# First tile re-planned and 512-byte q/k loads for two tiles of a fused attention and MLP kernel

## The chip, the cores and the metric

The kernel runs on one core of one Trainium2 chip. The metric is the device time of one execution in microseconds (us). The kernel before takes 272.12 us, the median of 13 runs (271.72 to 274.76).

## What is computed

For 4 batches, 8 heads, 768 tokens and a head width of 64, attention with a causal mask. Heads flagged in `is_retrieval` see all earlier keys, the others only the first 4 keys (sinks) and a window of 64. Its output, one row of 512 per token, goes through a layer of 2048 units with h - tanh(h) and back to 512.

```
scores = q @ k^T / 8;  stream_keep = causal & (is_sink | in_window)
scores = where(causal if head is retrieval else stream_keep, scores, -1e9)
x = softmax(scores) @ v                  # 3072 tokens x 512
h = x @ w_in                             # 3072 x 2048
out = (h - tanh(h)) @ w_out              # 3072 x 512, float32
```

## The kernel before, in words

Tokens are cut into 12 tiles of 256 (`TT`), three to a batch, and heads into 4 pairs. A unit n is one head pair of one tile. Each unit goes through these stages:

- `st_T`: TensorE transposes q and k of the pair into PSUM (`tp`, L487). One copy makes `qT`, two copies make the halves of `kz` (L473 on ScalarE, L475 on VectorE). `kz` is zero in the half that belongs to the other head, so it is cleared once (`zero_kz`, L349).
- `st_S`: scores into `sc` (L545), exp on ScalarE into `pt` (L560), and in the first group the mask on VectorE (L572 or L577: `pt` times `m4`).
- `st_A`: `pt` times values (L601), where key blocks further back than the previous one take `vf`, the values times the head's flag (L458, on GpSimd). Reciprocal and scaling on VectorE (L615, L620) give `x`.
- `st_X`: `x` transposed (L636) and copied to `xT` (L643).

The MLP of a tile has 8 units `H_unit(t, u)`: eight matmuls into `ph` (L663), tanh on ScalarE (L676), and the subtraction on VectorE (L683) into `gt`. `ph` has two banks, so the matmuls of unit u+2 wait for the subtraction of unit u. `O_mms` multiplies `gt` by `w_out` (L699) in groups of 16 matmuls, one group per 128 tokens, into `po`. ScalarE scales it out (L712), and SyncE (SP) stores it (L719). The output matmuls of tile t stand among the hidden units of tile t+1.

Loads: q, k and v come as float32, 256 bytes (one token of one head) to a packet (L253, on SP's queue), and are cast to 16 bits (L406 on ScalarE, L408 on VectorE or GpSimd). The six raw buffers are reused, so the loads of tile t+2 wait for the casts of tile t. The weights are loaded and cast by GpSimd's queue (L268, L280). Tiles 0 and 1 are loaded in halves of four heads.

Order: nothing is issued where it is written. Every operation is handed to `Plan.op` with an engine, a cost in ns, and what it reads and writes. `Plan.run` (L56) then plays these costs through: each engine takes, of what is ready, the operation that was recorded first. The operations are emitted in that order, and each engine runs them strictly in it. `port=True` marks operations that share GpSimd's port in the plan. A dependence named only for the plan (as `w_after` in the weight loads) makes no wait on the chip. On the chip an engine waits for the operations whose data it reads or overwrites; two readers of one tile in PSUM on different engines go one after the other as well.

The prologue stands at L748 to L781: casts of tile 0, its four units, casts of tile 1 (mostly GpSimd), the weight loads, `scale_v` (the `vf` products), and the clearing of the second `kz`. The main loop follows at L806: per hidden unit of tile t it places a share of the attention of later tiles. Tile 1's attention falls beside the hidden units of tile 0, when no output matmuls exist yet.

PSUM has eight banks: `sc` 2 x 2 banks (also used by `tp`), `m` 1 (`av`, `xp`), `h` 2 (`ph`), `o` 1 (`po`; `xp` in the prologue).

Of the kernel before, what the change touches and what calls it, by code (L numbers as in the profile page):

```python
# [16 lines left out]
class Plan:  # L17
# [3 lines left out]

    ENGINES = ("PE", "ACT", "DVE", "POOL", "SP")
    OVERLAP = {"PE": 0, "ACT": 100, "DVE": 88, "POOL": 60, "SP": 0}
    RESULT = {"PE": 200, "ACT": 0, "DVE": 0, "POOL": 0, "SP": 0}

    def __init__(self, bufs):
# [6 lines left out]
    def op(self, eng, ns, fn, r=(), w=(), dma=None, prio=None, port=False):  # L33
        i = len(self.ops)
        deps = set()
        for k in r:
            if k in self.writer:
                deps.add(self.writer[k])
            self.readers.setdefault(k, []).append(i)
        for k in w:  # L40
            if k in self.writer:
                deps.add(self.writer[k])
            deps.update(self.readers.get(k, ()))
            self.writer[k] = i
            self.readers[k] = []
        for key in (*r, *w):
            if isinstance(key, tuple) and key[0] in self.bufs:
                tag, at = key[:2]
                deps.update(self.users.get((tag, at - self.bufs[tag]), ()))
                self.users.setdefault((tag, at), []).append(i)  # L50
        deps.discard(i)
        port = port or (eng == "POOL" and not dma)
        self.ops.append((eng, ns, fn, deps, dma, i if prio is None else prio, port))
        return i
# [92 lines left out]
def kernel(  # L147
# [84 lines left out]
    raws = {}  # L232

    HH = H // 2

    def load(t, names="qkv", halves=(None,)):

        b, g = divmod(t, NG)
        for half in halves:
            h0, nh = (0, H) if half is None else (half * HH, HH)  # L240
            for nm in names:
                src = {"q": q, "k": k, "v": v}[nm]
                if (nm, t) not in raws:
                    idx = rot["raw"] = rot.get("raw", -1) + 1
                    raws[nm, t] = (
                        lazy(raw_pool, [128, NB, H, D], FP32, "raw", f"raw_{nm}{t}"), idx
                    )
                r, idx = raws[nm, t]
                for i in range(NB):
                    s0 = g * TT + i * 128  # L250
                    op(
                        "SP", max(420, 128 * nh * 1.1),
                        lambda r=r, i=i, src=src, s0=s0, h0=h0, nh=nh: nc.sync.dma_start(  # L253
                            out=r()[:, i, h0 : h0 + nh, :],
                            in_=src[b, h0 : h0 + nh, s0 : s0 + 128, :].rearrange("h p d -> p h d"),
                        ),
                        w=[("raw", idx, i, x) for x in (range(2) if half is None else (half,))],
                        dma=(128 * nh, 21.0),
                    )
# [16 lines left out]
    def load_w_out(j, w_after):  # L276
# [11 lines left out]

    retr_i = const.tile([128, 2 * H], I32, name="retr_i")
    op(  # L290
        "ACT", 400,
        lambda: nc.scalar.dma_start(
            out=retr_i[:], in_=is_retrieval.bitcast(I32).partition_broadcast(128)
        ),
        w=["retr"], dma=(128, 20.0),
# [55 lines left out]
        )  # L351

    for hp in range(HP):
        zero_kz("DVE", 0, hp, 0, S)

    nz = const.tile([128, 2 * H], FP32, name="nz")
    op(
# [52 lines left out]
    def cast_qk(t, engines, halves=range(2)):  # L410

        for half in halves:
            for nm, es in zip("qk", engines):
                if (nm, t) not in t16s:
                    t16s[nm, t] = lazy(
                        t16_pool, [128, NB, H, D], FP16, f"t16{nm}", f"t16_{nm}{t}"
                    )
                c = t16s[nm, t]
                r, slot = raws[nm, t]
                hs = slice(half * HH, half * HH + HH)  # L420
                cast_op(
                    es[half], NB * HH * D, lambda c=c, hs=hs: c()[:, :, hs, :],
                    lambda r=r, hs=hs: r()[:, :, hs, :],
                    r=[("raw", slot, i, half) for i in range(NB)], w=[("t16" + nm, t, half)],
                )

# [24 lines left out]
    def scale_v(t):  # L451
        b, g = divmod(t, NG)
        v1, vf, lo = v1s[b], vfs[b], g * NB
        for jb in range(lo, min(lo + NB, 4)):
            fl = rflag0 if jb == 0 else rflag
            op(
                "POOL", 1053,
                lambda jb=jb, fl=fl: nc.gpsimd.tensor_mul(  # L458
                    out=vf()[:, jb, :, :], in0=v1()[:, jb, :, :],
                    in1=fl[:].unsqueeze(2).to_broadcast([128, H, D + 1]),  # L460
                ),
                r=[("v1", b, g, 0), ("v1", b, g, 1), "rflag0", "rflag"], w=[("vf", b, jb)],
            )


# [5 lines left out]
    def copy(e, dst, src):  # L471
        if e == "ACT":
            nc.scalar.copy(out=dst, in_=src)  # L473
        else:
            nc.vector.tensor_copy(out=dst, in_=src)  # L475

    def st_T(n, eq="DVE", ek=("DVE", "DVE")):
        t, hp = divmod(n, HP)
        b, g = divmod(t, NG)
        cs = slice(g * TT, (g + 1) * TT)  # L480
        tp, key = bank([128, 2, NB, 128], FP16, "sc", f"tp{n}")
        cq, ck = t16s["q", t], t16s["k", t]

        def mm():
# [6 lines left out]

        op(
            "PE", 224, mm,
            r=["ident"] + [("t16" + nm, t, hp * 2 // HP) for nm in "qk"], w=[key],
        )
        qT[n] = lazy(qt_pool, [128, TT], FP16, f"qT{hp}", f"qT{n}")

        cost = {"ACT": 373, "DVE": 288}
        kk = kz[b % 2][hp]
        op(  # L500
            eq, cost[eq],
            lambda: copy(eq, qT[n]()[:], tp()[:, 0, :, :].rearrange("p i c -> p (i c)")),
            r=[key], w=[(f"qT{hp}", t)],
        )
        for hh in range(2):
            p_ = slice(64 * hh, 64 * hh + 64)
            op(
                ek[hh], cost[ek[hh]],
                lambda p_=p_, hh=hh: copy(
                    ek[hh], kk[p_, hh, cs], tp()[p_, 1, :, :].rearrange("p i c -> p (i c)")  # L510
                ),
                r=[key], w=[("kz", b % 2, hp, g)],
            )


# [137 lines left out]
    def H_unit(t, u):  # L653
# [33 lines left out]
            r=[key, tk], w=[("gt", t, u)],  # L687
        )

    def O_mms(t, j0, j1):  # L690
        for j in range(j0, j1, 2):
            ts, fb = divmod(j, NFB)
            if fb == 0:
                pos[t] = bank([128, DM], FP32, "o", f"po{t}_{ts}")
            po, key = pos[t]

            def mm(fb=fb, ts=ts, po=po):
                for f in (fb, fb + 1):
                    nc.tensor.matmul(  # L699
                        out=po()[:], lhsT=gts[t]()[:, f, ts * 128 : ts * 128 + 128],  # L700
                        rhs=w_out_t[f // 4]()[:, f % 4, :],
                        start=(f == 0), stop=(f == NFB - 1),
                    )

            op("PE", 2 * 216, mm, r=[("wout", fb // 4), ("gt", t, fb // FU)], w=[key])
            if fb == NFB - 2:
                ot = lazy(o_pool, [128, DM], FP32, "ot", f"ot{t}_{ts}")
                ok = ("ot", 2 * t + ts)
                t0 = t * TT + ts * 128
                op(  # L710
                    "ACT", 597,
                    lambda ot=ot, po=po: nc.scalar.activation(  # L712
                        out=ot()[:], in_=po()[:], func=AF.Copy, scale=1.0 / XS
                    ),
                    r=[key], w=[ok],
                )
                op(
                    "SP", 420,
                    lambda ot=ot, t0=t0: nc.sync.dma_start(out=out[t0 : t0 + 128, :], in_=ot()[:]),  # L719
                    r=[ok], dma=(128, 75.0),  # L720
                )


    NU = NTT * HP
# [20 lines left out]
            res.append(lambda: st_X(n))  # L745
        return res

    cast_qk(0, (("DVE", "DVE"), ("ACT", "DVE")), (0,))  # L748
    cast_v(0, ("POOL", "POOL"), (0,))
    cast_qk(0, (("DVE", "DVE"), ("DVE", "DVE")), (1,))  # L750
    cast_v(0, ("POOL", "POOL"), (1,))
    load(1, halves=range(2))
    for n in range(HP):
        st_T(n, "ACT", ("DVE", "ACT"))
        if n:
            for f in scores(n - 1):
                f()
        if n > 1:
            st_A(n - 2, 0)
            st_A(n - 2, 1)  # L760
        if n > 2:
            st_X(n - 3, "o")
    for f in scores(HP - 1):
        f()
    for n in (HP - 2, HP - 1):
        st_A(n, 0)
        st_A(n, 1)
        st_X(n - 1, "o")
    st_X(HP - 1, "o")
    for half in range(2):  # L770
        cast_qk(1, (("POOL", "POOL"), ("ACT", "POOL")), (half,))
        cast_v(1, ("POOL", "POOL"), (half,))
    for j in range(4):
        load_w_in(j, [("t16k", 1, 1)])
    load(2)
    scale_v(0)
    scale_v(1)
    for j in range(4):
        load_w_out(j, [("v1", 0, 1, 1)])
    for hp in range(HP):  # L780
        zero_kz("POOL", 1, hp, 0, S)  # L781

# [74 lines left out]
```

The softmax here doesn't subtract the row's maximum and nothing guards it: scores larger than these inputs give would overflow.

## Time and profile before

| What | Value |
|---|---|
| Time of the profiled execution | 272.12 us (span 270.3 us, so 1.8 us lie around it) |
| Median of 13 runs | 272.12 us |
| VectorE busy over the span | 174.0 us (64%) |
| ScalarE busy over the span | 156.8 us (58%) |
| GpSimd busy over the span | 71.5 us (26%) |
| Granted TensorE clock | full in all slices |
| Moved in the span | 29.78 MB in 82925 packets, 75728 of them under 512 B |
| First TensorE instruction | 9.1 us |

How to read it: TensorE (PE) runs 2560 matmuls, and a row for PE counts a matmul from its start to its modelled end, so matmuls overlap in it and a busy PE need not be at its peak. PEld is the weight load, which lies beside it. The rows by line give the number of instructions, their total and mean time, and what ended the idle time in front. In the timeline the first column is the start in us from the start of the span, the second the length, and the brackets give idle time and its releaser. The chain of waits follows the execution back from its last instruction.

### The profile page before, as it was taken

How to read it: one execution, taken by the hardware profiler on the slowest of the kernel's cores; microseconds unless marked ns; L12 is line 12 of the kernel's file. 1: busy time of each engine (PE TensorE's matmuls, PEld its weight loads, DVE VectorE, ACT ScalarE, POOL GpSimd, SP SyncE). 2: the span in 40 equal slices, each digit the busy share in tenths (PEclk: the TensorE clock that was granted, in tenths of full speed). 3: DMA queues.
4: the chain of work that ended last, by engine and by line, in shares of the span. 5: the costliest groups of instructions: out<-in, count | busy, mean ns of one | idle time of the engine just before them, and what ended most of it. 6: DMA issues, size and time to landing. Idle time of an engine off the chain costs nothing.

```text
span 270.3 us, 6313 instructions
## 1 busy us (share of the span) xinstructions
PE 249.1 (92%) x2560; PEld 187.3 (69%) x2560; DVE 174.0 (64%) x445; ACT 156.8 (58%) x228; POOL 71.5 (26%) x130
## 2 busy tenths in 40 slices
PE   0478879999999999999999999999999999999974
PEld 0356767777778877777777777777878777776631
DVE  7576765676898765567987646567887555554410
ACT  3355645875567777564577666654657766634420
POOL 7589201365641930309603000300300000000000
PEclk9999999999999999999999999999999999999999
DMA  7999999999999991175632511010001001010101
GB/s 151 219 216 204 197 196 201 216 230 199 251 228 192 190 184 55 45 154 133 140 79 62 100 40 40 2 41 39 19 22 41 2 39 41 1 42 39 41 39 78
DMA packets 82925, 29.78 MB, mean 110 GB/s; under 512 B 75728, under 2 KB 79824, under 8 KB 82896
## 3 DMA queue, kind: packets, MB, share of 16 engines
q1 hardware_dynamic: 78528, 25.17, 43.6%
q0 software_dynamic: 4224, 4.19, 9.2%
q8 instruction: 20, 0.33, 0.5%
q14 instruction: 9, 0.07, 0.1%
q10 hardware_dynamic: 144, 0.01, 0.0%
HBM read 27.27 MB, written 6.29 MB: 124 GB/s over the span
## 4 chain that ended last, share of the span: by engine, by line
PE 86%; DVE 7%; ACT 4%; issue 2%; DVEq 0%
PE po L699 30%; PE ph L663 29%; PE sc L545 14%; PE av L601 8%; PE tp L487 4%; ACT pt L560 2%; PE xp L636 2%; DVE gt L683 1%; DVE pt L572 1%; DVE kz L349 1%; DVE m L383 1%; ACT th L676 1%; DVE x L620 1%; ACT ot L712 1%; DVE nz L359 0%
## 5 line engine op out<-in xcount | busy, mean ns | idle before, releaser
L560 ACT ACTIVATE pt<-sc 128x1024 f16<-128x1024 f32 (+1 forms) x96 | 85.4, 915 | 28.2 <-PE sc L545 25.5
L663 PE MATMUL ph<-xT,win 128*128 128x256 f16 x768 | 100.7, 273 | 0.9 <-DVE gt L683 0.9
L699 PE MATMUL po<-wout,gt 128*128 128x512 f16 x384 | 100.3, 379 | 1.4 <-ACT ot L712 1.4
L676 ACT ACTIVATE th<-ph 128x512 f32<-128x512 f32 x96 | 57.4, 598 | 60.9 <-PE ph L663 57.3
L683 DVE SCALAR_TENSOR_TENSOR gt<-th,ph 128x512 f16<-128x512 f32 x96 | 65.7, 684 | 36.2 <-ACT th L676 35.5
L663 PEld LDWEIGHTS <-win 128*128 128x128 f16 x768 | 71.9, 98 | 14.1 <-issue 1.2
L545 PE MATMUL sc<-qT,kz 128*128 128x128 f16 (+1 forms) x448 | 54.1, 255 | 1.5 <-ACT kz L473 1.3
L699 PEld LDWEIGHTS <-gt 128*128 128x128 f16 x384 | 34.4, 98 | 23.1 <-issue 1.9
L545 PEld LDWEIGHTS <-kz 128*128 128x128 f16 x448 | 38.6, 101 | 13.8 <-issue 1.5
L601 PEld LDWEIGHTS <-pt 128*128 128x128 f16 x672 | 30.4, 99 | 7.6 <-DVE pt L572 1.7
L408 POOL CAST t_q<-raw_q 128x512 f16<-128x512 f32 x22 | 13.6, 629 | 81.8 <-issue 41.1
L601 PE MATMUL av<-v,pt 128*128 128x65 f16 x352 | 29.3, 198 | 0.8 <-DVE pt L572 0.7
L577 DVE TENSOR_TENSOR pt<-pt,m 128x1024 f16<-128x1024 f16 x32 | 22.8, 711 | 8.2 <-ACT pt L560 8.2
L475 DVE COPY kz<-tp 64x256 f16<-64x256 f16 x92 | 25.9, 283 | 2.2 <-ACT qT L473 1.1
L601 PE MATMUL av<-vf,pt 128*128 128x65 f16 x320 | 23.7, 194 | 1.0 <-DVE xT L475 1.0
L487 PE MATMUL tp<-ident,t_q 128*128 128x128 f16 x96 | 13.9, 229 | 10.0 <-DVE t_q L408 9.1
L712 ACT ACTIVATE ot<-po 128x512 f32<-128x512 f32 x24 | 14.3, 598 | 12.7 <-PE po L699 12.5
L615 DVE RECIPROCAL rinv<-av 128x4 f32<-128x4 f32 x48 | 8.6, 180 | 19.7 <-PE av L601 19.7
L620 DVE TENSOR_TENSOR x<-av,rinv 128x256 f16<-128x256 f32 x48 | 20.2, 422 | 1.3
L408 POOL CAST v<-raw_v 128x512 f16<-128x512 f32 x24 | 15.0, 647 | 20.2 <-DMA raw_v<-in_v_dram 20.2
L458 POOL TENSOR_TENSOR vf<-v,rflag 128x520 f16<-128x520 f16 x16 | 18.4, 1170 | 0.4
L487 PEld LDWEIGHTS <-t_q 128*128 128x128 f16 x96 | 8.8, 102 | 13.8 <-DVE t_q L408 9.1
(36 smaller groups left out, 122.5 us busy)
## 6 DMA issues: line engine op xcount, KB each, us to landing
out_dram<-ot SPq DMA_DIRECT2D x24, 256.0 KB, 2.1
raw_q<-in_q_dram SPq DMA_DIRECT2D x20, 256.0 KB, 4.3
raw_k<-in_k_dram SPq DMA_DIRECT2D x20, 256.0 KB, 4.7
raw_v<-in_v_dram SPq DMA_DIRECT2D x20, 256.0 KB, 4.3
win<-in_moe_w_in_dram POOLq DMA_DIRECT2D x4, 512.0 KB, 10.8
wout<-in_moe_w_out_dram POOLq DMA_DIRECT2D x4, 512.0 KB, 19.1
raw_q<-in_q_dram SPq DMA_DIRECT2D x8, 128.0 KB, 3.7
raw_k<-in_k_dram SPq DMA_DIRECT2D x8, 128.0 KB, 3.8
```

The lines of the kernel that those rows point to most:

```text
L408: op(e, cost, lambda: engs[e].tensor_copy(out=dst(), in_=src()), r=r, w=w, port=True)
L475: nc.vector.tensor_copy(out=dst, in_=src)
L487: nc.tensor.transpose(out=tp()[:, x, i, :], in_=c()[:, i, 2 * hp : 2 * hp + 2, :], identity=ident16[:],)
L545: nc.tensor.matmul(out=sc()[:, hh, o : o + nb * 128], lhsT=kk[:, hh, jb * 128 : jb * 128 + 128], rhs=qT[n]()[:, q0 * 128 : (q0 + nb) * 128 ...
L560: lambda: nc.scalar.activation(out=pt()[:, :, 512 * gi : 512 * gi + wid], in_=sc()[:, :, 0:wid], func=AF.Exp, scale=inv_sqrt_d,),
L577: nc.vector.tensor_mul(out=pv, in0=pv, in1=m4[:, hs, 256:512].unsqueeze(2).to_broadcast([128, 2, 2, 256]),)
L601: nc.tensor.matmul(out=av()[:, i, hh, :], lhsT=pt()[:, hh, co : co + 128], rhs=vv()[:, jb, h, :], start=(jb == 0), stop=(jb == qb),)
L620: lambda: nc.vector.tensor_mul(out=x16()[:], in0=av()[:, :, :, 0:D], in1=rinv()[:].unsqueeze(3).to_broadcast([128, NB, 2, D]),),
L663: nc.tensor.matmul(out=ph()[:, j, :], lhsT=w_in_t[fb // 4]()[:, cb, f0 : f0 + 128], rhs=xTs[t]()[:, cb, :], start=(cb == 0), stop=(cb == H ...
L676: lambda: nc.scalar.activation(out=th()[:], in_=ph()[:], func=AF.Tanh, scale=1.0 / XS),
L683: lambda: nc.vector.scalar_tensor_tensor(out=gts[t]()[:, u * FU : (u + 1) * FU, :], in0=th()[:], scalar=-XS, in1=ph()[:], op0=ALU.mult, op ...
L699: nc.tensor.matmul(out=po()[:], lhsT=gts[t]()[:, f, ts * 128 : ts * 128 + 128], rhs=w_out_t[f // 4]()[:, f % 4, :], start=(f == 0), stop=( ...
```

## The change

It consists of these parts:

1. **Loads.** q and k of tiles 0 and 1 come with tokens 2p and 2p+1 on partition p, so that a packet has 512 bytes, with one transfer per half instead of two. v and all later tiles stay as they are. After the transposes the tokens stand in even and odd blocks, and the copies to `qT` and `kz` of these two tiles put them back in order by reading the two blocks in turn.
2. **The flags** are loaded by SP, ahead of all else, and no longer by ScalarE's queue.
3. **Clearing of the first `kz`:** VectorE clears only the columns of tile 0 (256 of 768); GpSimd clears the rest, in the plan ahead of the second `kz`.
4. **Transposes:** q and k of a unit go to two different PSUM banks (in all tiles), and the plan learns that readers on two engines exclude each other.
5. **Prologue:** units 0 and 1 are begun before the second half of the casts; q of tile 0 is cast by ScalarE, k by VectorE; both k copies are on VectorE and the copy to `xT` on ScalarE; q and k of tile 1 are cast by ScalarE.
6. **`vf`** moves from GpSimd to VectorE, in all tiles, with a cost of 400 ns in the plan.
7. **Weights:** in the plan, w_in follows the cast of v of tile 1 half by half, and w_out follows the last w_in.
8. **The end:** the last tile's first output group uses bank `m`. Its last group is split into two halves of 256 columns, in `o` and `h`. The first is scaled out by ScalarE and stored from ScalarE's queue, the second by VectorE and stored by SP.

The diff, cut to its core:

```diff
+            if k[0] in self.PSUM:
+                deps.update(j for j in self.readers.get(k, ()) if self.ops[j][0] != eng)
...
+                if nm != "v" and t < PAIRED:
+                    op(
+                        "SP", max(420, 128 * nh * 1.1),
+                        lambda r=r, src=src, h0=h0, nh=nh: nc.sync.dma_start(
+                            out=r()[:, h0 : h0 + nh, :, :].rearrange("p h i d -> p h (i d)"),
+                            in_=src[b, h0 : h0 + nh, g * TT : g * TT + TT, :].rearrange(
+                                "h (p i) d -> p h (i d)", i=NB
+                            ),
+                        ),
...
-        "ACT", 400,
-        lambda: nc.scalar.dma_start(
+        "SP", 400,
+        lambda: nc.sync.dma_start(
...
-        zero_kz("DVE", 0, hp, 0, S)
+        zero_kz("DVE", 0, hp, 0, TT)
...
-                "POOL", 1053,
-                lambda jb=jb, fl=fl: nc.gpsimd.tensor_mul(
+                "DVE", 400,
+                lambda jb=jb, fl=fl: nc.vector.tensor_mul(
...
-        tp, key = bank([128, 2, NB, 128], FP16, "sc", f"tp{n}")
+        tp, key = bank([128, 2, 8, 128], FP16, "sc", f"tp{n}")
+        keys = [(*key, x) for x in range(2)]
...
+            if t < PAIRED:
+                return (
+                    dst.rearrange("p (c i) -> p c i", i=NB), src.rearrange("p i c -> p c i")
+                )
...
+            if t == NTT - 1 and ts == NB - 1:
+                if fb == 0:
+                    for f in range(0, NFB, 2):
+                        O_group(t, ts, f, f + 2, "o", 0, DM // 2, "ACT", "ACT")
+                    for f in range(0, NFB, 2):
+                        O_group(t, ts, f, f + 2, "h", DM // 2, DM, "DVE", "SP")
+                continue
+            O_group(t, ts, fb, fb + 2, "m" if t == NTT - 1 else "o")
...
-    cast_qk(0, (("DVE", "DVE"), ("ACT", "DVE")), (0,))
+    cast_qk(0, (("ACT", "ACT"), ("DVE", "DVE")), (0,))
+    load(1, halves=range(2))
+    for n in (0, 1):
+        st_T(n, "ACT", ("DVE", "DVE"))
+        for f in scores(n):
+            f()
     cast_v(0, ("POOL", "POOL"), (0,))
-    cast_qk(0, (("DVE", "DVE"), ("DVE", "DVE")), (1,))
-    cast_v(0, ("POOL", "POOL"), (1,))
-    load(1, halves=range(2))
-    for n in range(HP):
-        st_T(n, "ACT", ("DVE", "ACT"))
...
+    cast_qk(0, (("ACT", "ACT"), ("DVE", "DVE")), (1,))
+    for n in (0, 1):
+        st_A(n, 0)
+        st_A(n, 1)
+        st_T(n + 2, "ACT", ("DVE", "DVE"))
+        for f in scores(n + 2):
+            f()
+        st_X(n, "o", "ACT")
+    cast_v(0, ("POOL", "POOL"), (1,))
+    for n in (2, 3):
+        st_A(n, 0)
+        st_A(n, 1)
+        st_X(n, "o", "ACT")
+    for hp in range(HP):
+        zero_kz("POOL", 0, hp, TT, S)
     for half in range(2):
-        cast_qk(1, (("POOL", "POOL"), ("ACT", "POOL")), (half,))
+        cast_qk(1, (("ACT", "ACT"), ("ACT", "ACT")), (half,))
         cast_v(1, ("POOL", "POOL"), (half,))
     for j in range(4):
-        load_w_in(j, [("t16k", 1, 1)])
+        load_w_in(j, [("v1", 0, 1, j // 2)])
...
-        load_w_out(j, [("v1", 0, 1, 1)])
+        load_w_out(j, [("win", 3)])
```

`O_group` is the old body of `O_mms` with the bank, the columns, the engine and the queue as arguments; `store` is its end, and its scaling is planned at 110 ns plus 0.95 ns a column.

## Prediction

> **What bounds the kernel now.** I read the page first, then the pieces of the chain of waits, then the busy times by windows, then the timeline of both ends. The page's shares say that TensorE is the bound:
>
> ```profile
> PE 249.1 (92%) x2560; PEld 187.3 (69%) x2560; DVE 174.0 (64%) x445; ACT 156.8 (58%) x228; POOL 71.5 (26%) x130
> ```
>
> Busy time overlaps and runs, so I rebuild the need from pieces of the chain that have no gap:
>
> ```profile
> 49.04 0.87 PE ph L663 x8
> 49.91 0.77 PE sc L545 x10
> ...
> 53.09 0.67 PE av L601 x22
> ...
> 55.07 0.86 PE po L699 x4
> ```
>
> A matmul of 256 columns costs 0.109 us, of 512 0.215, of 128 0.056, of 65 0.030. Over all 2560 (768 ph, 384 po, 224 + 224 sc, 288 transposes, 672 av) that is 240.0 us. The other 30.3 us of the 270.3 us span lie as follows. 9.1 pass before the first matmul and 3.9 after the last one has been issued. Of the 17.4 between, counted from matmul starts, 15.1 lie before 40.7 us, 0.6 between 40.7 and 257, and 1.7 after. By 40.7 us only 16.5 us of needed work is done: 24.2 us are lost there. From then on TensorE has no holes worth naming, so only the first 40.7 us and the last 13 can give anything, and the middle can only lose. The windows show both stages (columns: PE, PEld, DVE, ACT, POOL, clock, DMA share, GB/s):
>
> ```profile
> 10.00:15.00 5.00, 3.19 (x25) 2.31 (x24) 2.56 (x8) 3.47 (x9) 4.14 (x5) 1.00 1.31 218
> ...
> 30.00:35.00 5.00, 4.73 (x58) 4.22 (x56) 3.94 (x10) 3.85 (x7) 1.25 (x2) 1.00 1.22 196
> 35.00:40.00 5.00, 4.18 (x48) 3.60 (x48) 3.17 (x9) 2.04 (x4) 0.00 (x0) 1.00 1.22 198
> ...
> 70.00:80.00 10.00, 10.00 (x108) 8.09 (x109) 8.87 (x26) 6.21 (x10) 5.13 (x8) 1.00 1.20 229
> ```
>
> Early on no engine is full: waits in chains set the pace. VectorE is 50 to 80% busy there, and reaches 89% at 70 to 80 us with TensorE full.
>
> **The head.** In the timeline the first transpose (9.10) waits for a cast that stands behind VectorE's masks:
>
> ```profile
> 3.33 2.09 POOL L349 MEMSET kz<- 128x768 f32 x3
> 4.28 1.17 DVE L359 TENSOR_SCALAR nz<-retr_i 128x16 f32<-128x16 int32 x1
> 5.96 2.74 DVE L383 TENSOR_SCALAR m<-A,thr 128x512 f16<-128x512 f16 x8
> 8.63 0.41 DVE L408 CAST t_q<-raw_q 128x512 f16<-128x512 f32 x1
> ```
>
> Data is not late (ScalarE casts k at 5.93). `nz` handles 16 numbers in 1.17 us and ends at 5.45, when GpSimd's clearing ends (5.42). The Trainium skill, SBUF — State Buffer, "Who interferes with whom", says why: a VectorE operation that uses two ports and a GpSimd operation exclude each other for one whole instruction. By that rule `nz` would have got in at 4.74, after the clearing then running (0.73 us each). The row is worse: VectorE waited through back-to-back clearings. This speaks against the change, which puts four clearings of 512 columns (0.49 each, from 0.73 x 512/768) on GpSimd.
>
> Worked by hand through the planner's costs, GpSimd's order becomes: one short clearing, two selects, three short ones, one long one, the cast of v, two long ones. The first run ends near 5.3, so `nz`, thr and the first mask come as before (5.8), although flags and `kz` come sooner. The eight masks at 0.26 reach to about 7.2 when v is cast (7.0 to 7.7). By the row, the last two then wait for the two long clearings (to 9.2), and the cast of k ends at 9.8. By the rule, one clearing at a time lets a mask in: 9.0 or less, 8.3 if the cast itself slips in. I take the row: first transpose at 9.8, 0.7 later; ends 8.3 and 10.2.
>
> **Loads.** 256-byte packets take 18 ns and the 2048-byte stores 84 in the DMA records; interpolated, 512 bytes take 27. A half of q or k (256 KB) then lasts 0.87 us instead of 1.17. Eight halves save 2.4 us by the end of tile 1 (last v lands at 15.7, not 17.9), and the flags ahead on SP cost 0.44 (the issue length of their row). As masks hide the first load, this brings nothing at the head; it only lets the weights start earlier, near 16 instead of 19.7. If that cover went, two halves less the 0.44 would be worth 0.2 at the head.
>
> **VectorE's work** from first transpose to 40.7 us is 22.0 us of these 31.6 (70%). The change:
>
> ```profile
> L620 DVE TENSOR_TENSOR x<-av,rinv 128x256 f16<-128x256 f32 x48 | 20.2, 422 | 1.3
> L577 DVE TENSOR_TENSOR pt<-pt,m 128x1024 f16<-128x1024 f16 x32 | 22.8, 711 | 8.2 <-ACT pt L560 8.2
> L458 POOL TENSOR_TENSOR vf<-v,rflag 128x520 f16<-128x520 f16 x16 | 18.4, 1170 | 0.4
> L475 DVE COPY kz<-tp 64x256 f16<-64x256 f16 x92 | 25.9, 283 | 2.2 <-ACT qT L473 1.1
> ```
>
> - `vf`, four here. 520 elements by the 16-bit row (1024 in 691 alone, 768 in 561) would be 0.43; by the rows with 32-bit inputs (256 in 0.42, 512 in 0.69) 0.70. The skill's VectorE: DVE Perf Modes, "The perf-mode tier table", gives two-tensor operations the double rate only in 16 bits, and the flags are float32. By the planner's 0.40, four cost 1.6; by the 32-bit rows 2.8. I take 2.8.
> - Copies of tiles 0 and 1 read two blocks in turn. The 0.283 row fits the double rate; one element a time, at the slope of the 32-bit rows (1.03 ns an element), adds half of 256 of these, 0.13 (estimate): 0.41. Bounds 0.28 and 0.41; I take 0.41. Tile 0 has eight on VectorE instead of four: +2.2. Tile 1 has twelve: +1.6.
> - Casts: one fewer after the first transpose, -0.4. Four xT copies to ScalarE: -1.1. Masks no longer held by GpSimd's `vf`: -0.2.
>
> Sum +4.9, so 26.9 us. ScalarE takes on q casts (2 x 0.62), tile 1's casts (4 x 0.62, formerly one) and xT (4 x 0.37), but gives up four k copies (1.5) and one k cast; at 40 to 77% busy it hides these. GpSimd loses casts and 4.7 us of `vf`, which nobody misses.
>
> **What is gained in the chain.** Before, one PSUM bank held q and k, so copies on two engines alternated: transposes ended at 9.72 and scores began at 11.46. In two banks, two k copies beside the q copy take 0.8 to 0.9: 0.8 us sooner. The fourth xT of tile 0 came at 22.66; by the same steps it comes 12.2 after the first transpose, near 22.0. The first hidden unit (29.77) stood in the order behind tile 1's attention because the plan expected w_in late; earlier due times move it forward some 4 us, and w_in lands in time (24.2 before). So chain waits shrink, and VectorE becomes the limit: 26.9 us at the 89% of the densest window is 30.2. First transpose 9.8 + 30.2 gives 40.0 for the end of holes, 0.7 us sooner than 40.7.
>
> **Middle.** Twelve `vf` add 8.4 us to VectorE under a full TensorE. VectorE is 69 to 89% busy until 80 us and less later, so most is hidden; uncovered, each would cost 0.7. I take +0.3 (0 to 1.5). The new PSUM rule in the plan changes no wait that the chip doesn't make: 0.
>
> **The end:**
>
> ```profile
> 256.92 1.03 PE L699 MATMUL po<-wout,gt 128*128 128x512 f16 x4
> ...
> 258.63 3.61 PE L699 MATMUL po<-wout,gt 128*128 128x512 f16 x16 [0.69 <-ACT ot L712]
> ...
> 262.93 3.61 PE L699 MATMUL po<-wout,gt 128*128 128x512 f16 x16 [0.69 <-ACT ot L712]
> 266.58 0.60 ACT L712 ACTIVATE ot<-po 128x512 f32<-128x512 f32 x1 [3.70 <-PE po L699]
> ```
>
> A group is 16 x 0.215 = 3.45. The first could start at 256.92 + 0.86 = 257.78 but waits for its bank until 258.63; the second repeats that (258.63 + 3.45 = 262.08). Bank `m` and the split remove both: -1.70; the subtraction that the group's last two matmuls need ends at 258.44, 3 us before them. 32 half matmuls are 3.49: +0.04. The last scaling is 256 columns on VectorE, 0.42 by the L620 row, for 0.60: -0.18. The last store (landed 2.0 us after) is half as long: 0 to -0.3, I take -0.15. ScalarE's own issue (0.44) has nothing behind it. Sum -2.0 (-1.7 to -2.2).
>
> **Total:** -0.7 + 0.3 - 2.0 = -2.4 against 272.12, which is both the time of the profiled execution (span 270.3 and 1.8 around it, taken as unchanged) and the median: **269.7 us**.
>
> **Rivals.**
> - *The prologue gives more (0.24):* GpSimd lets VectorE in, the first transpose is at 8.3, and VectorE is kept 95% full: 8.3 + 28.3 = 36.6, so -4.1 + 0.3 - 2.0 = 266.3. For it: 3.5 us earlier weights and dense hidden units. Against: the `nz` row.
> - *The start yields nothing (0.14):* loads were hidden anyway, and the holes end at 40.7 or a little later. Only the end is gained: 270.4, to 271.9 with the middle's 1.5.
> - *VectorE becomes the bound on the chain, slower (0.14):* in-order VectorE between the first transpose and the last early hidden unit. If it stays as gappy as now, its added work is added to the chain. At 75%, 26.9 us take 35.9, the holes end at 45.7: +5.0 + 0.3 - 2.0 = 275.4. It decides below 80% (holes ending after 43.2, which uses up the 1.7 + 0.8).
> - *Likeliest (0.48):* 269.7, itself 267.6 to 271.0.
>
> A measurement tells about 0.3% (0.8 us) from no change. Faster by that (below 271.3): all of the likeliest and the first, most of the second, 0.78; within 0.07; slower 0.15. Range 265.2 to 272.4, which leaves out the slower rival and the first rival's edge.
>
> **What would show it.** First matmul at 9.8, with masks held by clearings: right; at 8.3: the port was free. `vf` near 0.70 and paired copies near 0.41. VectorE over 85% busy between 10 and 40 us, last hole near 40. The end without `ot` waits, and the last matmul 1.7 us sooner relative to the last hidden unit. I am wrong if output matmuls wait for w_out, or VectorE's `vf` open holes after 50 us.

## The result, and the profile after

The changed kernel takes 274.5 us (median of 11 runs, 273.93 to 276.21) against 272.13 us (median of 48 runs of the kernel before): ratio 1.0092, 95% interval 1.0075 to 1.0109. It is slower by 2.4 us, where 2.4 us less had been forecast, and outside the range. The profiled execution took 275.05 us with a span of 273.3. Six of the 22 runs of one kernel below, e8, were in a slower state, and its ratio and median leave them out.

The page of the changed kernel, the line of busy times:

```profile
PE 249.4 (91%) x2576; PEld 187.7 (69%) x2576; DVE 185.8 (68%) x461; ACT 158.3 (58%) x232; POOL 51.7 (19%) x115
```

VectorE is busy 11.8 us longer. By the rows below, `vf` adds 11.0, the `kz` copies 3.4 (29.3 less the 25.9 of before) and the masks 3.1; what it gave up takes off the rest, 5.7.

Busy times by windows, same columns as before:

```profile
10.00:15.00 5.00, 1.78 (x10) 0.96 (x11) 3.02 (x7) 1.70 (x3) 2.84 (x12) 1.00 1.26 258
...
30.00:35.00 5.00, 4.37 (x54) 3.74 (x53) 4.00 (x10) 3.72 (x6) 0.00 (x0) 1.00 1.21 196
35.00:40.00 5.00, 4.46 (x71) 4.04 (x69) 4.40 (x12) 3.42 (x5) 1.64 (x3) 1.00 1.22 195
...
70.00:80.00 10.00, 9.65 (x99) 7.03 (x98) 9.47 (x27) 5.49 (x8) 3.73 (x6) 1.00 1.08 243
```

TensorE runs 10 matmuls from 10 to 15 us where it ran 25. At 70 to 80 us VectorE is 95% full, and TensorE, full before, is now busy for 9.65 of the 10 us.

The head, VectorE and GpSimd together, then TensorE and ScalarE (from the timeline):

```profile
5.26 0.73 POOL L370 MEMSET kz<- 128x768 f32 x1
5.27 5.83 DVE L404 TENSOR_SCALAR m<-A,thr 128x512 f16<-128x512 f16 x8 [0.43 <-POOL A L334]
...
7.08 0.61 POOL L429 CAST v<-raw_v 128x512 f16<-128x512 f32 x1 [1.10 <-DMA raw_v<-in_v_dram]
7.64 2.09 POOL L370 MEMSET kz<- 128x768 f32 x3
...
11.02 0.41 DVE L429 CAST t_k<-raw_k 128x512 f16<-128x512 f32 x1
11.48 0.40 PE L512 MATMUL tp<-ident,t_k 128*128 128x128 f16 x2 [5.51 <-DVE t_k L429]
11.91 0.37 ACT L497 COPY qT<-tp 128x256 f16<-128x256 f16 x1 [6.39 <-PE tp L512]
12.32 0.88 DVE L499 COPY kz<-tp 64x256 f16<-64x256 f16 x2 [0.89 <-ACT qT L497]
...
14.21 0.88 DVE L499 COPY kz<-tp 64x256 f16<-64x256 f16 x2 [1.02 <-PE tp L512]
15.18 0.37 ACT L497 COPY qT<-tp 128x256 f16<-128x256 f16 x1 [0.58 <-DVE kz L499]
```

Two things are to be seen. The eight masks take 5.83 us instead of 2.74, and while they do, GpSimd casts v and clears. One of the eight, alone in the timeline from 7.2 to 9.7 us, takes 2.77 us:

```profile
7.10 2.77 DVE L404 TENSOR_SCALAR m<-A,thr 128x512 f16<-128x512 f16 x1
```

That is the length of the cast of v (7.08) and the three clearings behind it (to 9.73). TensorE has q's transposes done at 5.97, as ScalarE now casts q; the transpose of k waits 5.51 us for the cast behind the masks. And the two kinds of copies still go one after the other: at 12.32 `kz` has waited 0.89 for `qT`, at 15.18 `qT` waits 0.58 for `kz`.

Rows by line, with their shapes:

```profile
L499 DVE COPY kz<-tp 64x256 f16<-64x256 f16 x96 | 29.3, 306 | 3.9 <-ACT qT L497 1.5 <-PE tp L512 1.0
...
L482 DVE TENSOR_TENSOR vf<-v,rflag 128x520 f16<-128x520 f16 x16 | 11.0, 716 | 0.1
...
L404 DVE TENSOR_SCALAR m<-A,thr 128x512 f16<-128x512 f16 x8 | 5.8, 796 | 0.4 <-POOL A L334 0.4
```

`vf` costs 0.716 as forecast (0.70); two `kz` copies in 0.88 us are 0.43 each (forecast 0.41).

The end, in the timeline:

```profile
262.07 7.97 PE L756 MATMUL po<-wout,gt 128*128 128x512 f16 x52
...
268.33 0.38 ACT L732 ACTIVATE ot<-po 128x256 f32<-128x256 f32 x1 [1.15 <-PE po L756]
270.14 0.42 DVE L736 TENSOR_SCALAR ot<-po 128x256 f32<-128x256 f32 x1 [6.55 <-PE po L756]
```

The 52 output matmuls (of 512 and, at the end, 256 columns) run without a stop; both waits for `ot` are gone.

To say where the time went, I took each gap from one matmul's start to the next, less the time that the first one needs (the four durations of the prediction; 239.8 us in all). These are the lost microseconds by stage, with the time before the first matmul in the first column of losses:

| Kernel | First k transpose | Fourth xT of tile 0 | First hidden unit | Lost to 25 us | 25 to 50 | 50 to 250 | From 250 | After the last matmul |
|---|---|---|---|---|---|---|---|---|
| before | 9.29 | 22.66 | 29.77 | 19.43 | 4.81 | 0.71 | 1.71 | 3.92 |
| after | 11.48 | 27.97 | 27.26 | 21.61 | 5.24 | 3.25 | 0.03 | 3.42 |

Start (the two columns to 50 us) +2.6, middle +2.5, end -2.2: +3.0 in sum, the difference of the spans (273.3 less 270.3); the medians differ by 2.4. In the middle the 2.5 are mostly two gaps, 0.52 at 75.0 and 1.62 at 131.4:

```profile
127.29 1.13 DVE L482 TENSOR_TENSOR vf<-v,rflag 128x520 f16<-128x520 f16 x1
...
128.65 0.68 DVE L717 SCALAR_TENSOR_TENSOR gt<-th,ph 128x512 f16<-128x512 f32 x1
...
129.25 1.91 DVE L482 TENSOR_TENSOR vf<-v,rflag 128x520 f16<-128x520 f16 x3
...
131.08 0.96 DVE L606 TENSOR_TENSOR pt<-pt,m 128x768 f16<-128x768 f16 x1
...
132.63 0.41 DVE L654 TENSOR_TENSOR x<-av,rinv 128x256 f16<-128x256 f32 x1
...
133.10 0.28 PE L670 MATMUL xp<-ident,x 128*128 128x128 f16 x2 [1.46 <-DVE x L654]
```

Four `vf` stand almost in a row on VectorE; the scaling that makes `x` is behind them, and TensorE waits 1.46 us for it.

### The profile page after: what moved, and what is told of

Its sections match the earlier page's. It is cut to its first block, busy times and chain, and to the rows that moved or that the text cites. A ratio compares the mean times of both kernels' runs of the same rounds, so it can differ in the third digit from the quotient of the medians.

```text
span 273.3 us, 6343 instructions
## 1 busy us (share of the span) xinstructions
PE 249.4 (91%) x2576; PEld 187.7 (69%) x2576; DVE 185.8 (68%) x461; ACT 158.3 (58%) x232; POOL 51.7 (19%) x115
## 4 chain that ended last, share of the span: by engine, by line
PE 83%; DVE 11%; ACT 2%; DMA 1%; issue 1%; POOL 0%; DVEq 0%; ACTq 0%
PE po L756 29%; PE ph L697 28%; PE sc L579 14%; PE av L635 7%; PE tp L512 3%; DVE m L404 2%; PE xp L670 2%; DVE kz L499 2%; DVE gt L717 2%; DVE vf L482 2%; ACT pt L594 1%; DMA retr_i<-in_is_retrieval_dram 1%; DVE x L654 1%; DVE pt L606 1%; DVE qT L499 1%
## 5 line engine op out<-in xcount | busy, mean ns | idle before, releaser
L697 PE MATMUL ph<-xT,win 128*128 128x256 f16 x768 | 103.1, 274 | 0.7 <-DVE gt L717 0.5
L756 PE MATMUL po<-wout,gt 128*128 128x512 f16 (+1 forms) x400 | 100.2, 370 | 0.0
L756 PEld LDWEIGHTS <-gt 128*128 128x128 f16 x400 | 35.8, 98 | 19.6
L579 PEld LDWEIGHTS <-kz 128*128 128x128 f16 x448 | 37.2, 99 | 15.5 <-DVE kz L499 3.9
L499 DVE COPY kz<-tp 64x256 f16<-64x256 f16 x96 | 29.3, 306 | 3.9 <-ACT qT L497 1.5
L429 POOL CAST t_q<-raw_q 128x512 f16<-128x512 f32 x20 | 12.2, 617 | 89.9 <-issue 82.2
L611 DVE TENSOR_TENSOR pt<-pt,m 128x1024 f16<-128x1024 f16 x32 | 22.2, 694 | 7.7 <-ACT pt L594 7.7
L732 ACT ACTIVATE ot<-po 128x512 f32<-128x512 f32 (+1 forms) x24 | 14.1, 589 | 10.6 <-PE po L756 10.5
L512 PE MATMUL tp<-ident,t_k 128*128 128x128 f16 x96 | 14.0, 230 | 5.5 <-DVE t_k L429 5.5
L499 DVE COPY qT<-tp 128x256 f16<-128x256 f16 x44 | 13.0, 295 | 6.2 <-PE tp L512 6.2
```

Of the source, the lines that this page charges most:

```text
L429: op(e, cost, lambda: engs[e].tensor_copy(out=dst(), in_=src()), r=r, w=w, port=True)
L512: nc.tensor.transpose(out=tp()[:, x, i, :], in_=c()[:, i, 2 * hp : 2 * hp + 2, :], identity=ident16[:],)
L579: nc.tensor.matmul(out=sc()[:, hh, o : o + nb * 128], lhsT=kk[:, hh, jb * 128 : jb * 128 + 128], rhs=qT[n]()[:, q0 * 128 : (q0 + nb) * 128 ...
L611: nc.vector.tensor_mul(out=pv, in0=pv, in1=m4[:, hs, 256:512].unsqueeze(2).to_broadcast([128, 2, 2, 256]),)
L697: nc.tensor.matmul(out=ph()[:, j, :], lhsT=w_in_t[fb // 4]()[:, cb, f0 : f0 + 128], rhs=xTs[t]()[:, cb, :], start=(cb == 0), stop=(cb == H ...
L756: nc.tensor.matmul(out=po()[:, c0:c1], lhsT=gts[t]()[:, f, ts * 128 : ts * 128 + 128], rhs=w_out_t[f // 4]()[:, f % 4, c0:c1], start=(f == ...
```

## The experiments

Theory: the slowdown is two additions on VectorE, masks stopped by GpSimd's clearings in the head (about 1.7 us) and `vf` in its order in the middle (about 2.5); the end gained what was forecast; and the re-planned start is worth little by itself. Rivals: it is the start's new order and not the clearings; it is VectorE's sum and not the place of `vf`; the loads or the banks cost something.

| Kernel | Median us | Ratio to before, 95% | First k transpose | Lost to 25 us | 25 to 50 | 50 to 250 |
|---|---|---|---|---|---|---|
| e1 kz on VectorE | 273.35 | 1.0032 (1.0017 to 1.0048) | 8.93 | 20.65 | 3.84 | 3.27 |
| e2 vf on GpSimd | 272.7 | 1.001 (0.9989 to 1.003) | 10.56 | 21.44 | 5.32 | 1.20 |
| e3 both | 270.11 | 0.9928 (0.9905 to 0.995) | 8.93 | 20.35 | 4.06 | 0.35 |
| e4 the end alone | 270.13 | 0.9931 (0.991 to 0.9952) | 9.30 | 19.42 | 4.84 | 0.72 |
| e5 k in a tile of its own | 269.01 | 0.9882 (0.9854 to 0.991) | 8.80 | 18.92 | 4.98 | 0.35 |
| e6 masks late | 268.85 | 0.9886 (0.9869 to 0.9903) | 6.52 | 19.83 | 2.80 | 0.95 |
| e7 flags in 16 bits | 273.69 | 1.0053 (1.0035 to 1.0071) | 9.00 | 20.96 | 5.21 | 2.84 |
| e8 end and paired loads | 269.0 | 0.9876 (0.9854 to 0.9898) | 8.07 | 19.21 | 2.97 | 1.90 |
| e9 clearings later | 273.36 | 1.0044 (1.0032 to 1.0057) | 7.56 | 20.32 | 3.88 | 4.08 |
| e10 vf priced at 700 ns | 271.08 | 0.996 (0.9942 to 0.9977) | 8.92 | 20.92 | 4.10 | 1.16 |
| b1 = e3 + e5 + e6 | 265.59 | 0.9778 (0.9753 to 0.9803) | 6.52 | 16.83 | 2.94 | 0.65 |
| b2 loads, e5, e6 in the old start | 268.71 | 0.9878 (0.9863 to 0.9893) | 6.90 | 18.55 | 2.90 | 2.20 |

The stages are those of one profiled execution each; the medians stand on several. The profiled execution of the changed kernel is 0.55 us above its median, that of e1 0.64 below, so stages of two kernels compare to about 1 us. In e5 (38.5 to 41.9 us), b2 (23.9 to 27.3) and e8 (19.0 to 25.8) the granted clock drops to 0.50, and part of the time lost there is the clock's, not the edit's.

### e1, e2 and e3: the two suspects, each and together

```diff
-        zero_kz("DVE", 0, hp, 0, TT)             # e1, e3
+        zero_kz("DVE", 0, hp, 0, S)
...
-    for hp in range(HP):
-        zero_kz("POOL", 0, hp, TT, S)
...
-                "DVE", 400, ... nc.vector.tensor_mul(     # e2, e3
+                "POOL", 1053, ... nc.gpsimd.tensor_mul(
```

> The kernel after, with the first kz cleared whole by VectorE again, so GpSimd has four clearings instead of eight, all before the cast of v. Theory P (back-to-back clearings on GpSimd hold the masks, which hold the cast of k): the eight masks take about 2.7 us instead of 5.8, the first k transpose comes at about 9 instead of 11.5, and the time falls by 1.5 to 2.5 us, to about 272.5. Theory V (the added vf and slower copies on VectorE set the pace from 10 to 45 us, whatever the head does): the masks are quicker but the end of the early holes stays near 45 us, and the time stays within 0.8 us of 274.5.

> The kernel after, with vf on GpSimd again. Theory V: the holes at 75 us (0.9) and 131 us (1.7) go, and the prologue gains up to 2.8 us of VectorE time; the time falls by 2.5 to 4.5 us, to 270 to 272. Theory P: only the two middle holes go, 2.5 us at most; the start stays as late as it is, about 272.0.

> The kernel after with both undone: kz cleared by VectorE, vf on GpSimd. If both theories hold and add, about 274.5 - 2.0 - 2.5 = 270.0, which is 272.1 less the 2.1 of the end. Below 269.5: the rest of the new prologue is worth something. Above 271: the rest of the new prologue costs (copies of two blocks, casts of tile 1 on ScalarE).

Undone alone, the clearing gives back 1.15 us (1.5 to 2.5 expected) and `vf` 1.8 (2.5 expected); undone together 4.4, more than the sum and about as expected, and the gain over the kernel before is then 2.0. In e2 the middle's loss falls from 3.25 to 1.20, in e3 to 0.35. The head of e3 on VectorE, in the timeline:

```profile
5.67 2.87 DVE L404 TENSOR_SCALAR m<-A,thr 128x512 f16<-128x512 f16 x8
8.46 0.41 DVE L429 CAST t_k<-raw_k 128x512 f16<-128x512 f32 x1
...
9.77 0.42 DVE L499 COPY kz<-tp 64x256 f16<-64x256 f16 x1 [0.89 <-ACT qT L497]
```

The masks take half the time that they took in the changed kernel, and the cast follows 2.6 us sooner; the wait of 0.89 between the copies stays. Why the two effects more than add was not tried. At the start e1, with `vf` on VectorE, loses 24.49 us and e3, without it, 24.41: `vf` is not shown to cost anything there. (Single executions scatter: e7, which differs from e1 only in the flags, loses 26.17.)

### e4: the end alone, in the kernel before

The edit is the change's `store`, `O_group` and `O_mms` put into the kernel before, and nothing else.

> The kernel before with the new end alone. By the sum for the end: 2.0 us less, 270.1 (269.9 to 270.4). If the last store or the split costs what the waits gave, it stays at 272.

270.13 us: the forecast's term of -2.0 alone would have given 270.1. Its end in the timeline:

```profile
256.94 7.97 PE L722 MATMUL po<-wout,gt 128*128 128x512 f16 x52
...
265.01 0.42 DVE L702 TENSOR_SCALAR ot<-po 128x256 f32<-128x256 f32 x1 [6.55 <-PE po L722]
```

And e3, which keeps all else of the change, is no faster than this (270.11). So the new start, with loads, banks and the earlier hidden units, is worth nothing measurable in sum; gains and losses inside it may cancel.

### e5: k's transposes in a PSUM tile of their own

The change puts q and k into two banks of one tile. This takes a second tile for k in tile 0:

```diff
+        if t == 0:
+            tkb, kkey = bank([128, NB, 128], FP16, "h", f"tk{n}")
+            keys[1] = (*kkey, 0)
...
-                        out=tp()[:, x, i, :], ...
+                        out=(tk()[:, i, :] if x else tp()[:, x, i, :]), ...
```

> Built on the kernel with kz on VectorE and vf on GpSimd (270.1). In the first tile the k transposes go to a PSUM tile of their own (bank h, free then), instead of the second bank of one tile. If the copies of q and k alternate because both read one tile, although in two banks, the k copies start beside the q copy here and each of the four units is 0.4 to 0.8 us shorter: 1 to 2 us less, 268.5 to 269. If the alternation is not on the path, 270.1 stays.

1.1 us less than e3; the two intervals just touch, so that the size is rough. In its timeline the copies stand beside one another:

```profile
8.80 0.39 PE L517 MATMUL tk<-ident,t_k 128*128 128x128 f16 x2 [2.76 <-DVE t_k L429]
...
9.23 0.42 DVE L499 COPY kz<-tk 64x256 f16<-64x256 f16 x1 [0.49 <-PE tk L517]
9.45 0.37 ACT L497 COPY qT<-tp 128x256 f16<-128x256 f16 x1 [0.65 <-PE tp L517]
...
10.02 2.31 DVE L499 COPY kz<-tk 64x256 f16<-64x256 f16 x5
```

The copy of k starts before that of q and runs beside it; five k copies follow without a stop. The fourth `xT` of tile 0 comes at 22.23 instead of 26.21. In the changed kernel the copy of k is released by ScalarE's copy of q, here by TensorE's `tk`. So it is the tile that the wait goes by, not the bank. Whether the chip itself would let two engines read two banks of one tile at once was not tried.

### e6: at most two masks ahead of the first cast of k

```diff
-    for h in range(H):
+    masks(0, 2)
...
+        masks(2, 4, [("kz", 0, 0, 0)])      # after unit 0
...
+        masks(4, H, [("kz", 0, 1, 0)])      # after unit 1
```

The names in brackets are waits in the plan only.

> Built on the kernel with kz on VectorE and vf on GpSimd (270.1). Only the first pair's masks stand ahead of the cast of k, the other six follow the first copies. If the head is what costs, the first k transpose comes at about 6.7 us instead of 8.9 and 1.5 to 2 us are won: about 268.3. If what is won at the head is lost again in waits behind it (for data, for ScalarE, for VectorE), the early holes end where they ended and 270.1 stays.

In the trace one mask runs ahead of the cast (5.78 and 6.05 us) and the second behind it. The first transpose of k comes 2.4 us before that of e3, and the whole kernel is 1.3 us shorter: half of what is won at the head arrives.

### e7 and e10: why `vf` hurts

e7 is e1 with the flags copied to 16 bits, which the forecast had named as the reason for the single rate:

```diff
+    f16 = const.tile([128, 2, H], FP16, name="f16")
...
-            fl = rflag0 if jb == 0 else rflag
+            fl = f16[:, 0, :] if jb == 0 else f16[:, 1, :]
```

> Built on the kernel with kz on VectorE alone (273.35, vf on VectorE with float32 flags at 0.70). The flags are copied to 16 bits first. If the rate of vf is set by the width of its inputs, vf takes about 0.43 and four in a row 1.6 instead of 2.6; the holes at 73 and 129 us shrink by half or more, and the time falls by 1 to 2.5 us, to about 271.5. If the repeated operand forbids the double rate, vf stays at 0.70 and 273.3 stays.

Its row by line:

```profile
L491 DVE TENSOR_TENSOR vf<-v,f 128x520 f16<-128x520 f16 x16 | 10.9, 718 | 0.1
```

718 ns with 16-bit flags, 716 without: the width of the flags decides nothing. The operand that is left is the repeated one (a flag stands for 65 columns); that it is the cause is argued by exclusion, not shown. e10 is e1 with `vf` at 700 ns instead of 400 in the plan, so that the work is the same and only the order differs.

> The kernel with the first kz cleared by VectorE (273.35), with vf on VectorE planned at its measured 700 ns instead of 400. If the holes at 73 and 129 us come from the planner's wrong price, they shrink and the time falls by 1 to 2.5 us, to 271 to 272.4. If they come from four operations of 0.7 us in a row on a busy in-order engine, whatever the plan believes, 273.3 stays within 0.7.

271.08 against 273.35 us of e1, the loss in the middle 1.16 against 3.27. VectorE in the same stretch:

```profile
124.51 1.13 DVE L482 TENSOR_TENSOR vf<-v,rflag 128x520 f16<-128x520 f16 x1
...
126.47 1.30 DVE L482 TENSOR_TENSOR vf<-v,rflag 128x520 f16<-128x520 f16 x2
...
129.03 0.41 DVE L654 TENSOR_TENSOR x<-av,rinv 128x256 f16<-128x256 f32 x1
...
129.56 0.68 DVE L482 TENSOR_TENSOR vf<-v,rflag 128x520 f16<-128x520 f16 x1
```

The four `vf` are now spread, with `x` between them. So most of the middle's cost was the wrong price in the plan, not the 0.7 us each. What is left of `vf` on VectorE is about 1.0 us (e10 less e3).

### e9: the same eight clearings, later

```diff
-        zero_kz("POOL", 0, hp, TT, S)
+        zero_kz("POOL", 0, hp, TT, S, [("v1", 0, 0, 1)])
...
-        zero_kz("POOL", 1, hp, 0, S)
+        zero_kz("POOL", 1, hp, 0, S, [("wout", 3)])
```

> The kernel after with the same eight clearings on GpSimd, but ordered behind the casts of v of tile 0 (the first four) and behind the last of w_out in the plan (the other four), so that none stands beside the masks. If the clearings' place beside the masks is what costs, the eight masks take 2.2 to 2.9 us instead of 5.8, the first k transpose comes near 8.5, and the time is at most that of the kernel with the first kz cleared by VectorE (273.35; 272.8 to 273.5). If it is the amount of clearing on GpSimd that costs, wherever it stands, 274.5 stays.

GpSimd does all the clearing of the changed kernel, but not beside the masks (timeline):

```profile
4.97 2.19 DVE L404 TENSOR_SCALAR m<-A,thr 128x512 f16<-128x512 f16 x8 [0.43 <-POOL A L334]
7.08 0.42 DVE L429 CAST t_k<-raw_k 128x512 f16<-128x512 f32 x1
7.18 0.78 POOL L429 CAST v<-raw_v 128x512 f16<-128x512 f32 x1 [2.25 <-DMA raw_v<-in_v_dram]
```

2.19 us for eight masks, 0.27 each, against 5.83. The time is that of e1 (273.36 and 273.35): the place of the clearings cost 1.1 us, not their amount. The first transpose of k is 3.9 us earlier than in the changed kernel, of which 1.1 arrive.

### e8: the paired loads without the new start

e4 with the 512-byte loads and the copies that put the tokens back in order.

> The kernel before with the new end (270.13), and of the rest only the loads of 512 bytes for q and k of tiles 0 and 1, with the copies that put the tokens in order. If the loads are hidden and only the copies count (0.13 more on each of some 20 on VectorE), 270.1 to 271.5. If earlier data and weights count for more, 268.5 to 270.

By the ratios it is 0.5% below e4 (0.9876 against 0.9931, intervals apart), 1.5 us; by the medians 1.1. The loads can't be given all of that: here GpSimd's third clearing moved from before 5.4 us to 8.24, `nz` took 0.17 us at 4.61 instead of 1.18 at 4.28, and the masks 2.19 instead of 2.75, so the first transpose of k came at 8.07:

```profile
4.61 0.17 DVE L377 TENSOR_SCALAR nz<-retr_i 128x16 f32<-128x16 int32 x1 [0.25 <-DMA retr_i<-in_is_retrieval_dram]
...
5.30 2.19 DVE L401 TENSOR_SCALAR m<-A,thr 128x512 f16<-128x512 f16 x8
```

How much is left for the packets is open.

### b1 and b2: what the findings add up to

b1 is e3 with the edits of e5 and e6; b2 puts the paired loads, k's own tile and the late masks into the start of the kernel before.

> Both winners on the new prologue: kz on VectorE, vf on GpSimd, k transposes of the first tile in a PSUM tile of their own, and only the first pair's masks ahead of the cast of k. Alone they gave 269.0 and 268.9 over 270.1. If both gains come from the same waits, 268.5; if they add, 267.6.

> The kernel before with the new end and the 512-byte loads (269.8), and the same two changes in its own prologue (k transposes of the first tile apart, masks of the first pair first). If what they give does not depend on the new prologue, 267.3 to 268.7; if the old prologue hides them, 269 to 270.

b1 takes 265.59 us (265.19 to 267.31), 2.2% less than the kernel before, 8.9 us less than the changed one, and 2.0 less than expected had the two gains added. b2 stays at 268.71, the upper edge of what was expected. The head of b1 in its timeline:

```profile
5.77 0.35 DVE L406 TENSOR_SCALAR m<-A,thr 128x512 f16<-128x512 f16 x1
6.04 0.42 DVE L433 CAST t_k<-raw_k 128x512 f16<-128x512 f32 x1
...
6.52 0.39 PE L521 MATMUL tk<-ident,t_k 128*128 128x128 f16 x2 [0.48 <-DVE t_k L433]
...
6.95 1.32 DVE L503 COPY kz<-tk 64x256 f16<-64x256 f16 x3 [0.23 <-PE tk L521]
```

The cast follows the first mask, and three k copies run through. So the new start (its order, with the flags on SP's queue and the plan's new rule and due times) is worth 3.1 us over the old one (b1 against b2), but only once nothing holds its first steps. By the table about half of that lies behind 50 us (0.65 against 2.20); what causes that part is open. e5 and e6 gave 1.1 and 1.3 alone and 4.5 together; that they more than add is measured, the reason is not settled (the clock below is a candidate).

## Why the prediction was wrong, point by point

- **First transpose at 9.8: too early, 11.48** (of k, which was meant; q's came at 5.58). The mechanism was right, and the row was the better guide than the rule: the Trainium skill (SBUF — State Buffer, "Who interferes with whom") has the shared ports held for one whole instruction, which the forecast read as letting a mask in after each clearing; in the trace one mask waited through the cast of v and three clearings (2.77 us). The size failed in the order worked out by hand: three long clearings stood behind the cast of v (7.64 to 9.73), not two, one more ran at the start of the masks (5.26), and a second cast of v (10.02) held the last mask. Eight masks took 5.83 us; the forecast's order amounts to some 3.6 (5.8 to 9.4). e9 shows the cause: with the clearings elsewhere the masks take 2.19 us. `nz`, from which the row came, was itself not held this time (0.17 us at 3.92).
- **Two banks, 0.8 us sooner: failed.** The copies alternated as before, because waits between readers go by PSUM tile, as the section on the kernel before has it; the forecast took the bank for the tile. "By the same steps it comes 12.2 after the first transpose" became 16.5 (11.48 to 27.97), against 13.4 before. With a tile for k the copies overlap and the kernel is 1.1 us shorter (e5).
- **"Chain waits shrink, and VectorE becomes the limit: 26.9 us at the 89% of the densest window": this is the step on which the sign turned.** The start was to give 0.7 us and cost 2.6. With the start as forecast the sum would have been -0.7 + 2.5 - 2.2 = -0.4; with the middle as forecast it would have been 2.6 + 0.3 - 2.2 = +0.7. The terms of its work were right: `vf` 11.0 us over the span (11.2 forecast), `kz` copies +3.4 (+3.8). But it was busy 27.2 of the 35 us from 10 to 45, 78% (23.8 before), and never near 89%: the waits stayed, those behind the masks (e9) and between the copies (e5). The rival "VectorE becomes the bound on the chain, slower" named this, with a threshold of 80% and 275.4 us. Its sign and, by luck, its total came true; its split did not, +5.0 at the start where +2.6 was measured, +0.3 in the middle where it was +2.5.
- **Half speed was left out.** The forecast took all of the 24.2 us lost ahead of 40.7 as waits. In the kernel before, TensorE ran at about half speed until 25.4 us (last section). The 5.8 us of needed work until then took some 5 us more for that (an estimate from starts 1.9 times as far apart); no term of the forecast has them.
- **Middle +0.3 (0 to 1.5): mis-sized, +2.5.** That each uncovered `vf` costs 0.7 was right. What was missed: the plan priced it at 400 ns, and so put four in a row ahead of `x`. e10 shows it.
- **The reason for 0.70** (flags in 32 bits) was wrong, the number right: e7.
- **First hidden unit four us sooner:** 2.5 sooner (27.26), although the fourth `xT` came 5.3 later (27.97 against 22.66).
- **Loads:** hidden behind the masks, as forecast: k's cast stood behind the masks until 11.02, while ScalarE had q's data at 4.90. The interpolated 27 ns for a packet of 512 bytes was too low: 32 in the records of the changed kernel (median; 18 for 256 bytes). For e8 it is open. **ScalarE** was busy 1.5 us more over the span; that this cost nothing is not shown.
- **Two figures do not come out of their own lines.** By the windows VectorE's work from 9.1 to 40.7 us is 21.2 us (67%), not 22.0, which would have moved the forecast some 0.9 us further down; and 22.66 less 9.10 less 0.8 is 12.8, not the 12.2 for the fourth `xT`, which stands in no total.
- **The end, -2.0 (-1.7 to -2.2):** right. e4 gives -2.0; by the table the two waits account for 1.7 and the shorter last scaling and store for 0.5.

## What to carry to other kernels

Work moved to an engine with idle time is nearly free only if the plan that orders that engine knows its price: here the wrong price cost 2.3 us (e1 less e10), where 0.3 had been put down for the whole move. Before counting on two engines side by side, look in the trace for which tile their waits go by, and before handing fills to GpSimd, look at what VectorE does at that moment. A gain at the head arrives only in part until the next stop behind it is gone as well: transposes that came 2.4 and 3.9 us sooner brought 1.3 and 1.1 (e6, e9), and e5 and e6 gave about 1 us each, together 4.5.

## What the runs showed of the hardware

- VectorE's masks wait through a run of GpSimd's clearings: eight take 2.19 us with GpSimd idle beside them (e9), 2.87 with one cast of v beside them (e3), and 5.83 with two such casts and four clearings (after). A single mask waited 2.77 us through one cast and three clearings that followed without a pause.
- A product with a repeated operand takes 0.72 us for 520 columns whether the flags have 32 or 16 bits. The Trainium skill (VectorE: DVE Perf Modes, "What auto-detection actually checks") asks for a step of one element besides the 16 bits, which a repeated flag does not have; e7's 718 ns agree with that, but no run took the repetition alone away.
- TensorE runs at about half speed early on. The profile's rows show a granted clock of 1.00 there, but the trace holds no clock record before the full speed begins. Two transposes of 128 columns in the changed kernel, early and late:

```profile
13.54 0.42 PE L512 MATMUL tp<-ident,t_q 128*128 128x128 f16 x2
...
125.97 0.28 PE L512 MATMUL tp<-ident,t_q 128*128 128x128 f16 x2
```

Their starts lie 0.105 us apart early and 0.056 late. The full speed begins at 25.4 us before, 28.8 after, 28.0 in e1, 31.0 in e7, 28.2 in e3, 24.9 in e5 and 21.3 in b1. The work done until then needs 5.0 to 7.3 us at full speed, so nearly as much again goes to the slow stretch. What ends it was not tried. This may be why a transpose that comes 2.5 us sooner brings only 1.1: more of the work runs slowly (5.9 us in e1, 5.0 in the changed kernel). No run took the slow stretch away, so its share is not measured. It can come back: in e5 TensorE stood idle for 2.52 us, waiting for a cast on GpSimd, and the granted clock (third number from the right) was 0.50 from 38.5 us on, with half speed behind it:

```profile
38.50:41.90 3.40, 3.06 (x20) 2.36 (x21) 0.97 (x4) 0.64 (x1) 0.84 (x2) 0.50 1.21 194
```
